# Regrouping products and visits at the start, one ScalarE step, and the conversion of w_out, in a fused retention and SiLU kernel

## The chip, the cores and the metric

The kernel runs on one core of a Trainium2 chip. The metric is the device time of one execution in microseconds; the median of 9 runs of the kernel before is 630.65 us (628.59 to 632.96). Profiles show one execution: TensorE is PE (its weight loads PEld), VectorE DVE, ScalarE ACT, GpSimd POOL, and SyncE (SP) issues most DMAs.

## What is computed

```python
for t in range(S):                       # B, H, S, D = 4, 8, 768, 64
    state = gamma[None, :, None, None] * state + einsum('bhd,bhe->bhde', k[:, :, t], v[:, :, t])
    y[:, :, t] = scale * einsum('bhd,bhde->bhe', q[:, :, t], state)
x = y.transpose(0, 2, 1, 3).reshape(B * S, H * D)      # 3072 x 512
h = x @ w_in                                           # 512 x 2048
out = (h * (1.0 / (1.0 + exp(-h)))) @ w_out            # 2048 x 512
```

The weights arrive as 64-bit floats and are converted in the kernel. Both large matrix products are made of three products of rounded parts (high by high, high by low and a mixed plane), so each has three planes of x or g and three of w.

## The kernel before

**Chunks and units.** The sequence of 768 is cut into NC = 6 chunks of 128 steps. A unit is one chunk of one batch, so there are 24 units, numbered chunk by chunk (unit 4c + b).

**Visits.** `visit(m)` (L535) works on three units at once. For unit m it transposes k and q on PE (`stage_t`, 8 transposes into the PSUM tiles kp and qp, copied out by ACT, L400). For unit m-1 it makes the chunk's sums of k and v (`stage_s`, L414) and the scores (`stage_a`, L424) in the PSUM tile sc. DVE then masks the scores (am, L432), adds up the state (mid, L441 and state, L445) and scales q (L365). For unit m-2 it makes y: the products with the masked scores first, then with the states, in two parts (`stage_y`, L457); a memset on POOL fences the two parts (`fence`). y is copied out of its one PSUM tile by ACT (ys, L492) and split into the three planes of xt (ACT L504, DVE L507, L508). At its end a visit issues the loads of later units on SP. From visit 2B + 1 = 9 on q and k of later units are loaded into rings of two or three buffers; from visit 17 the transposes run on DMA instead. One visit has 240 matmul and weight-load instructions for chunk 0 and 272 later.

**Products.** `product_in(c, f)` (L581) multiplies chunk c of x (all four batches, 512 columns) by slice f of 16 of w_in: 8 matmuls into ha and 4 into hb. ha and hb take turns on three PSUM banks, so hb of a product uses the bank of ha of the product before, and ha of a product that of hb two products before. Behind each product ACT copies ha into g (L589), DVE subtracts hb (L593, the product's sum), ACT applies SiLU (L597), and SP writes g to DRAM (gd). `behind_copy` and `behind_next` are lists of work that is issued behind a product's copy and behind its sum.

**Weights.** `take_w` converts the next of 32 slices (0 to 15 of w_in, 16 to 31 of w_out): ACT L197 (ca), DVE L199 (cs), L201 (ca), L204 (cs), L206 and L208 (cp), L214 (the sum cs, or cw for w_out). A slice of w_in is then split into three planes by `split_w`: ACT L119, DVE L122 (wil), ACT L124, DVE L125. A slice of w_out is written to DRAM (wod, L236), read back in the last group (wr, L622), and split there by `w_out` with the same four steps (wo, wol). The raw slices (wf, loaded two ahead, when the slice two before is converted) and the read-back slices (wr) share one ring of two tiles, `stage`; the tile wl serves both cw and wol. `begin_w` and `end_w` make the two halves of such a conversion inside the visits from 6 on.

**Order.** The order on PE is written by hand (L652 and after). On the other engines the order is fixed when the kernel is built, by the framework's scheduler, and each engine keeps it. By hand the order is: visits 0 to 9, with slice 0 taken behind visit 3, product (0,0) behind visit 7 and (0,1) behind visit 9; then the list `steps` of products, and in `behind` what follows each: visits 10, 11, 12 behind (1,0), (1,1), (1,2), visit 13 behind (1,3). Later visits stand behind every fourth product. Products of chunks 3, 4 and 5 make groups 3, 4 and 5. `takes` says behind which products slices are converted. A second phase (L718 and after) multiplies g, read back and split, by the planes of w_out: 6 chunks of 16 steps of 12 matmuls, 2.72 us a step.

Of the kernel before, what the change touches and what calls it, by code (L numbers as in the profile page):

```python
# [2 lines left out]

# [1 line left out]

# [27 lines left out]
def kernel(  # L33
# [29 lines left out]
    B, H, S, D = q.shape  # L63
# [5 lines left out]
    NF = DF // 128  # L69
# [43 lines left out]
    def split_w(f, w32, name, factor, to):  # L113


        to[f] = w = w_slot(f, name)
        lo = conv.tile([128, 512], FP32, tag="wl", name=f"{name}l_{f}")
        with tc.issue_after(held[0] if f >= NF - 4 else evac[0]):
            nc.scalar.activation(out=w[:, 0, :], in_=w32, func=AF.Copy, scale=HALF * factor)  # L119
        high = w[:, 0, :].bitcast(FP32)  # L120
        yield
        nc.vector.scalar_tensor_tensor(out=lo, in0=w32, scalar=factor, in1=high,  # L122
                                       op0=ALU.mult, op1=ALU.subtract)
        nc.scalar.activation(out=w[:, 1, :], in_=lo, func=AF.Copy, scale=1.0 / EPS)  # L124
        nc.vector.scalar_tensor_tensor(out=w[:, 2, :], in0=high, scalar=EPS, in1=lo,  # L125
                                       op0=ALU.mult, op1=ALU.subtract)


    units = [(c, b) for c in range(NC) for b in range(B)]
    kqv = {"k": {}, "q": {}, "v": {}}  # L130
    EARLY = 2 * B
# [90 lines left out]
    def take_w(after=None, parts=False):  # L222

        i = taken[0]
        taken[0] += 1
        if i >= 2 * NF:
            return
        with tc.issue_after(after) if after else ExitStack():
            rounded = convert_w(i)

        def finish():
            w32 = rounded()
            if i < NF:
                list(split_w(i, w32, "wi", scale, w_sb))
            else:
                nc.sync.dma_start(out=wo_dram[i - NF], in_=w32)  # L236

        if parts:
            behind_next.append(finish)
        else:  # L240
            with tc.issue_after(after) if after else ExitStack():
                finish()

    def end_w():

        while half_split:
            list(half_split.pop())
# [69 lines left out]
    behind_next, behind_copy, half_split = [], [], []  # L317
# [44 lines left out]
    def scale_q(n):  # L362
        c, b = units[n]
        t, g = (x if c > 0 else x[:, :, D:] for x in (qt[n], gq))
        nc.vector.tensor_tensor(out=t, in0=t, in1=g, op=ALU.mult)  # L365
# [25 lines left out]
    def stage_t(n):  # L391

        for name, to, bufs, src, tp in (
                ("kt", kt, 2, kqv["k"][n], turn(f"kp_{n}")),
                ("qt", qt, 3, kqv["q"].pop(n), banks("q", f"qp_{n}", 1)[:, 0])):
            tp = tp.rearrange("p (a t) -> p a t", a=HP)
            for a in range(HP):
                nc.tensor.transpose(tp[:, a, :], src[:, 2 * a : 2 * a + 2, :], ident)  # L398
            to[n] = one.tile([128, HP, C], FP32, tag=name, name=f"{name}_{n}", bufs=bufs)
            evac[:] = [nc.scalar.copy(out=to[n], in_=tp).ins]  # L400

    def score_tile(n):
        u = banks("s", f"sc_{n}")
        sc, sums = (u[:, :, ts(i, 4 * D)].rearrange("p o (a t) -> p o a t", a=HP)
                    for i in range(2))
        return sc, sums
# [40 lines left out]
    def stage_y(n):  # L447

        vs, amn, qtn = kqv["v"].pop(n), am.pop(n), qt.pop(n)
        states = steps_of.pop(n)  # L450
        yp = banks("y", f"y_{n}")[:, :, : 4 * D].rearrange("p o (a t) -> p o a t", a=HP)

        started, done, new = set(), [], []

        def product(a, o, j, lhsT, rhs):
            e = j ^ (a % 2)
            i = nc.tensor.matmul(yp[ts(e, D), o, a, :], lhsT=lhsT, rhs=rhs,  # L457
                                 start=(e, o) not in started, stop=True,
                                 skip_group_check=True).ins
            started.add((e, o))  # L460
            if new:
                fence(done[-1], i)
                new.clear()
            done.append(i)

        def scores():
            for a in range(HP):
                for o in range(2):
                    for j in range(2):
                        product(a, o, j, vs[ts(o, D), 2 * a + j, :], amn[ts(o, D), j, a, :])  # L470

        def states_with(part):

            new.extend([part] * part)
            for a in range(HP):
                for o in range(2):
                    j = o ^ part
                    if states[o] is not None:
                        product(a, o, j, states[o][ts(j, D), a, :], qtn[ts(j, D), a, ts(o, D)])

        return scores, states_with, yp
# [52 lines left out]

    def visit(m):  # L535

        first, mid, last = (0 <= m - i < len(units) for i in range(3))
        if first and m < FAR:
            stage_t(m)
        if last:  # L540
            scores, states_with, yp = stage_y(m - 2)
            scores()
        if mid:
            sc, sums = score_tile(m - 1)
            stage_s(m - 1, sums)
        if last:
            states_with(0)
        if mid:
            stage_a(m - 1, sc)
            if m > 1 and units[m - 1][1] == 0:  # L550
                next_chunk()

            with tc.issue_after(taken_out[0]) if m > 3 * B + 1 else ExitStack():
                finish_a(m - 1, sc, sums)
            scale_q(m - 1)
        if m == 0:
            chunk_decays()
            first_chunk()
        if first and m < FAR:
            scale_k(m)  # L560
        if last:
            states_with(1)
            finish_y(m - 2, yp)

        if FAR <= m < len(units):
            with tc.issue_after(fenced[0]):
                part_t(m)
        for name in "kqv":
            for n in (m + 1, m + 2):
                if n >= EARLY and n == (m + 1 if name == "v" or n > FAR else m + 2):  # L570
                    load(name, n)
        if EARLY - 2 <= m < 3 * B + 2:
            with tc.issue_after(masked[0]):
                end_w()
                if m not in (EARLY - 1, EARLY + 1):
                    begin_w()
# [4 lines left out]
    def product_in(c, f):  # L581
        ha, hb = turn(f"ha_{c}_{f}"), turn(f"hb_{c}_{f}")
        for i in range(3):
            for kk in range(KIN):
                nc.tensor.matmul(hb if i == 2 else ha, lhsT=w_sb[f][:, i, ts(kk, 128)],  # L585
                                 rhs=xt[c][:, i, kk, :], start=kk == 0 and i != 1,
                                 stop=kk == KIN - 1 and i != 0)
        hs = hpool.tile([128, NT], FP32, tag="hs", name=f"g_{c}_{f}")
        copied[:] = [nc.scalar.activation(out=hs, in_=ha, func=AF.Copy, scale=ONE_E).ins]  # L589
        with tc.issue_after(copied[0]):  # L590
            while behind_copy:
                behind_copy.pop(0)()
        taken_out[:] = [nc.vector.tensor_tensor(out=hs, in0=hs, in1=hb, op=ALU.subtract).ins]  # L593
        with tc.issue_after(taken_out[0]):
            while behind_next:
                behind_next.pop(0)()
        nc.scalar.activation(out=hs, in_=hs, func=AF.Silu)  # L597
        pending.append((c, f, hs))
# [52 lines left out]

    ctx.enter_context(tc.manual_schedule(engines={mybir.EngineType.PE}))  # L652

    for m in range(EARLY + 2):
        visit(m)
        if m == 3:
            take_w()
        elif m == EARLY - 1:
            load_w(3)
            product_in(0, 0)  # L660
        elif m == EARLY + 1:
            product_in(0, 1)

    half = NF // 2
    pairs = [(1, 0), (1, 1)] + [(c, f) for f in range(2, 4) for c in range(2)]
# [3 lines left out]
    last = ([(c, f) for c in range(2) for f in range(NF - 4, NF)] +  # L669
            [(2, f) for f in range(half, NF)])  # L670
    groups = [(c, f) for c in range(3, NC) for f in range(NF)]
    steps = pairs + three + rest + last + groups
    takes = [(0, f) for f in range(5, half)]
    takes += [(2, half - 4), (2, half - 2)]
    takes += [(0, half), (0, half + 2), (1, half), (1, half + 2)]
    takes += [(0, NF - 4), (0, NF - 2), (2, half + 2), (2, half + 4)]
    takes += [(c, f) for c in (3, 4) for f in (0, 3, 6, 8, 11, 14)]
    behind = {(1, f): lambda f=f: visit(EARLY + 2 + f) for f in range(3)}
    behind[1, 3] = lambda: [visit(3 * B + 1), behind_next.append(end_w)]
    at = ([(1, NF - 1)] + [(2, f) for f in range(NF - 7, NF - 2, 2)] +  # L680
          [(c, 4 * i + 1) for c in range(3, NC - 1) for i in range(B)])
# [36 lines left out]
    for c in range(NC):  # L718
# [8 lines left out]
        for f in range(NF):  # L727
# [5 lines left out]
            first_, last = f == 0, f == NF - 1  # L733
# [57 lines left out]
```

## Time and profile before

| | us |
|---|---|
| median of 9 runs | 630.65 |
| the profiled execution | 630.81 |
| its span, first to last instruction | 629.0 |

Busy time in stretches of the span:

| stretch | what runs | PE busy | DVE busy | ACT busy |
|---|---|---|---|---|
| 0 to 66 | visits 0 to 10, three products | 49.49 | 45.61 | 42.92 |
| 66 to 132 | visits 11 to 13, products | 65.74 | 58.08 | 51.40 |
| 132 to 205 | products, the first late visits | 72.37 | 62.96 | 44.94 |
| 205 to 318 | late visits, groups 3 and 4 | 111.54 | 91.85 | 69.25 |
| 318 to 362 | group 5 | 44.00 | 33.60 | 34.49 |
| 362 to 629 | second phase | 262.27 | 133.61 | 68.97 |

In the first stretch PE is idle for 16.5 us, in all others together for 7. The granted clock of PE is full but for one window in the first stretch. A line of the chain of waits gives start, length, and the work or wait that carried the end; a line of a stretch gives for each engine its busy time and, behind x, its instructions.

### The profile page before, as it was taken

Reading aid. Unit: us, or ns where it says so; the run is one execution under the profiler, and the core shown is the slowest. Engines: PE = TensorE matmul, PEld = TensorE weight load, DVE = VectorE, ACT = ScalarE, POOL = GpSimd, SP = SyncE. Lnnn points to the kernel's source line nnn. Section 1 sums busy time; section 2 is a strip of 40 time slices with the busy share of each in tenths; the row PEclk is TensorE's granted clock in tenths of the full one; section 3 lists DMA queues with packets and bytes.
Section 4 is the critical chain, followed back from the end, with each engine's and each line's share of the span. In section 5 each row is a group of like instructions: output and inputs, shape, how many; then the busy total and the mean of one; then the engine's idle time right before and its main releaser. Section 6 shows DMA issues by size and latency. Waiting matters only on the chain.

```text
span 629.0 us, 13483 instructions
## 1 busy us (share of the span) xinstructions
PE 605.4 (96%) x5384; PEld 499.8 (79%) x5384; DVE 425.7 (68%) x732; ACT 312.0 (50%) x583; POOL 23.4 (4%) x79
## 2 busy tenths in 40 slices
PE   5788999999999999999999999999999999999997
PEld 3677788887888787888788888888888888888785
DVE  2798898798978888897697583553636454554631
ACT  5567896666655566667478761312312221412211
POOL 3000000000000211111000000000000000000000
PEclk9998999999999999999999999999999999999999
DMA  9996887445667799999856553342533433432301
GB/s 199 209 212 165 225 231 228 168 150 192 196 202 200 191 271 252 258 269 263 290 188 207 178 168 100 119 149 68 169 99 106 163 95 106 136 132 96 106 1 67
DMA packets 137998, 107.31 MB, mean 171 GB/s; under 512 B 94800, under 2 KB 103248, under 8 KB 137936
## 3 DMA queue, kind: packets, MB, share of 16 engines
q1 hardware_dynamic: 135056, 101.21, 57.0%
q10 hardware_dynamic: 2880, 5.24, 2.2%
q8 instruction: 42, 0.69, 0.5%
q14 instruction: 20, 0.16, 0.1%
HBM read 66.06 MB, written 36.70 MB: 163 GB/s over the span
## 4 chain that ended last, share of the span: by engine, by line
PE 84%; DVE 6%; DMA 3%; issue 2%; ACT 2%; SPq 2%; DVEq 0%; ACTq 0%; POOLq 0%
PE ha L585 23%; PE o L740 20%; PE oa L740 14%; PE hb L585 12%; PE ob L740 7%; PE y L457 4%; PE sc L424 1%; PE sc L414 1%; SPq L149 1%; PE qp L398 1%; DMA qw<-qp 1%; DMA kqv<-in_q_dram 1%; DMA wf<-in_moe_w_in_dram 1%; PE kp L398 1%; DMA wod<-cw 1%
## 5 line engine op out<-in xcount | busy, mean ns | idle before, releaser
L585 PE MATMUL ha<-xt,wi 128*128 128x512 f32 x768 | 192.7, 393 | 0.0
L585 PEld LDWEIGHTS ha<-xt,wi 128*128 128x128 f32 x768 | 142.8, 188 | 30.9 <-DVE g L593 0.4
L740 PE MATMUL o<-wo,gs 128*128 128x512 f32 x576 | 146.2, 389 | 0.0
L740 PEld LDWEIGHTS o<-wo,gs 128*128 128x128 f32 x576 | 108.1, 188 | 22.4
L642 DVE TENSOR_TENSOR gs<-gr,gs 128x512 fp32r<-128x512 f32 x96 | 62.1, 685 | 90.8 <-ACT gs L640 90.8
L640 ACT ACTIVATE gs<-gr 128x512 fp32r<-128x512 f32 x96 | 53.4, 621 | 134.7 <-issue 132.3
L740 PE MATMUL oa<-wo,gs 128*128 128x512 f32 x384 | 118.2, 389 | 0.0
L585 PE MATMUL hb<-xt,wi 128*128 128x512 f32 x384 | 103.1, 390 | 1.5 <-ACT g L589 1.4
L593 DVE TENSOR_TENSOR g<-g,hb 128x512 f32<-128x512 f32 x96 | 65.6, 683 | 36.7 <-ACT g L589 23.2
L585 PEld LDWEIGHTS hb<-xt,wi 128*128 128x128 f32 x384 | 71.8, 188 | 17.7 <-ACT g L589 2.2
L740 PEld LDWEIGHTS oa<-wo,gs 128*128 128x128 f32 x384 | 72.1, 188 | 14.9
L597 ACT ACTIVATE g<-g 128x512 f32<-128x512 f32 x96 | 60.5, 631 | 41.8 <-DVE g L593 41.6
L740 PE MATMUL ob<-wo,gs 128*128 128x512 f32 x192 | 75.2, 392 | 0.3 <-DVE o L749 0.3
L589 ACT ACTIVATE g<-ha 128x512 f32<-128x512 f32 x96 | 56.6, 589 | 25.7 <-PE ha L585 12.1
L643 DVE SCALAR_TENSOR_TENSOR gs<-gs 128x512 fp32r<-128x512 f32 x96 | 61.9, 683 | 0.0
L740 PEld LDWEIGHTS ob<-wo,gs 128*128 128x128 f32 x192 | 36.0, 188 | 9.3 <-DVE o L749 2.0
L197 ACT ACTIVATE ca<-wf 128x512 f32<-128x512 f32 x32 | 21.6, 676 | 16.0 <-DVE cs L204 6.1
L208 DVE SCALAR_TENSOR_TENSOR cp<-wf,cp 128x512 f32<-128x512 uint32 x32 | 23.5, 734 | 0.6
L457 PE MATMUL y<-qt,mid 64*64 64x64 f32 x384 | 21.9, 230 | 2.0 <-issue 2.0
L204 DVE SCALAR_TENSOR_TENSOR cs<-ca,cs 128x512 uint32<-128x512 uint32 x32 | 22.1, 690 | 0.9
L748 ACT ACTIVATE o<-o 128x512 f32<-128x512 f32 x10 | 6.0, 598 | 33.4 <-PE o L740 33.0
L432 DVE TENSOR_TENSOR am<-sc,decay 128x512 f32<-128x512 f32 x24 | 16.4, 684 | 8.8 <-PE sc L424 8.7
(84 smaller groups left out, 557.9 us busy)
## 6 DMA issues: line engine op xcount, KB each, us to landing
gd<-g SPq DMA_DIRECT2D x96, 256.0 KB, 3.1
gr<-gd SPq DMA_DIRECT2D x96, 256.0 KB, 2.7
wf<-in_moe_w_out_dram SPq DMA_DIRECT2D x16, 512.0 KB, 4.4
out_dram<-o ACTq DMA_DIRECT2D x20, 256.0 KB, 2.1
wf<-in_moe_w_in_dram SPq DMA_DIRECT2D x16, 256.0 KB, 3.9
wf<-in_moe_w_in_dram SPq DMA_DIRECT2D x32, 128.0 KB, 4.0
kf<-in_k_dram SPq DMA_DIRECT2D x16, 256.0 KB, 4.8
qf<-in_q_dram SPq DMA_DIRECT2D x16, 256.0 KB, 4.3
```

The costliest lines, as they stand in the source:

```text
L197: nc.scalar.activation(out=a.bitcast(FP32), in_=hi.bitcast(FP32), func=AF.Abs, scale=65536.0)
L204: nc.vector.scalar_tensor_tensor(out=s, in0=a, scalar=3, in1=s, op0=ALU.logical_shift_left, op1=ALU.bitwise_or)
L208: nc.vector.scalar_tensor_tensor(out=p.bitcast(FP32), in0=lo, scalar=2.0 ** -52, in1=p.bitcast(FP32), op0=ALU.mult, op1=ALU.mult)
L457: i = nc.tensor.matmul(yp[ts(e, D), o, a, :], lhsT=lhsT, rhs=rhs, start=(e, o) not in started, stop=True, skip_group_check=True).ins
L585: nc.tensor.matmul(hb if i == 2 else ha, lhsT=w_sb[f][:, i, ts(kk, 128)], rhs=xt[c][:, i, kk, :], start=kk == 0 and i != 1, stop=kk == KIN ...
L589: copied[:] = [nc.scalar.activation(out=hs, in_=ha, func=AF.Copy, scale=ONE_E).ins]
L593: taken_out[:] = [nc.vector.tensor_tensor(out=hs, in0=hs, in1=hb, op=ALU.subtract).ins]
L597: nc.scalar.activation(out=hs, in_=hs, func=AF.Silu)
L640: nc.scalar.activation(out=t[:, 0, :], in_=g, func=AF.Copy, scale=HALF)
L642: nc.vector.tensor_tensor(out=t[:, 1, :], in0=g, in1=high, op=ALU.subtract)
L643: nc.vector.scalar_tensor_tensor(out=t[:, 2, :], in0=t[:, 1, :].bitcast(FP32), scalar=-1.0 / EPS, in1=high, op0=ALU.mult, op1=ALU.add)
L740: nc.tensor.matmul(o, lhsT=g, rhs=wo[f][:, i, :], start=first_ and i != 1, stop=last and i != 0)
```

## The change

Four edits. A visit is written as a generator of two halves, `halves(m)`: the first has the transposes, y's products with the scores and the first part of those with the states; the second has the rest. In every visit `stage_s` thereby moves behind the first part of the states. The start is reordered: slice 0 is taken behind visit 2 instead of 3, product (0,0) stands behind visit 6 instead of 7, and from visit 9 halves and products alternate: 9a, (0,1), 9b, 10a, (1,0), 10b, (1,1), 11a, (0,2), 11b, (1,2), 12a, (0,3), 12b, (1,3), 13. The step to the next chunk's decay (`next_chunk`, four ACT operations) is issued, in late visits, behind the copy of the next product and a unit earlier. And slices are taken behind other products: four of w_in's and all of w_out's, whose last twelve are spread over groups 3, 4 and 5 as 5, 4 and 3 instead of over groups 3 and 4 as 6 and 6.

```diff
     def visit(m):
+        list(halves(m))
+    def halves(m):
         first, mid, last = (0 <= m - i < len(units) for i in range(3))
         if first and m < FAR:
             stage_t(m)
         if last:
             scores, states_with, yp = stage_y(m - 2)
             scores()
+            states_with(0)
+        yield
         if mid:
             sc, sums = score_tile(m - 1)
             stage_s(m - 1, sums)
-        if last:
-            states_with(0)
-        if mid:
             stage_a(m - 1, sc)
-            if m > 1 and units[m - 1][1] == 0:
+            if 1 < m <= 3 * B + 1 and units[m - 1][1] == 0:
                 next_chunk()
...
             scale_q(m - 1)
+            if m > 3 * B + 1 and units[m - 1][1] == B - 1:
+                behind_copy.append(next_chunk)
...
-    for m in range(EARLY + 2):
+    for m in range(EARLY + 1):
         visit(m)
-        if m == 3:
+        if m == 2:
             take_w()
+        elif m == EARLY - 2:
+            product_in(0, 0)
         elif m == EARLY - 1:
             load_w(3)
-            product_in(0, 0)
-        elif m == EARLY + 1:
-            product_in(0, 1)
+    half_visits = (x for m in range(EARLY + 1, 3 * B + 1) for x in chain(halves(m), (None,)))
+    next(half_visits)
+    product_in(0, 1)
+    next(half_visits)
+    next(half_visits)
...
-    takes += [(0, half), (0, half + 2), (1, half), (1, half + 2)]
-    takes += [(0, NF - 4), (0, NF - 2), (2, half + 2), (2, half + 4)]
-    takes += [(c, f) for c in (3, 4) for f in (0, 3, 6, 8, 11, 14)]
-    behind = {(1, f): lambda f=f: visit(EARLY + 2 + f) for f in range(3)}
+    takes += [(0, half), (0, half + 3), (1, half + 1), (1, half + 3)]
+    takes += [(0, NF - 2), (2, half), (2, half + 2), (2, half + 4)]
+    takes += [(3, f) for f in (0, 3, 7, 11, 14)]
+    takes += [(4, f) for f in (3, 7, 11, 14)]
+    takes += [(5, f) for f in (1, 3, 5)]
+    behind = {x: lambda: next(half_visits) for x in pairs[:-1]}
```

More of the change, by code (lines that the diff above doesn't have):

```diff
@@ L2 @@
 from contextlib import ExitStack
+from itertools import chain
 import numpy as np
```

## The prediction

> **What bounds the kernel now.** The page comes first: 605.4 us of TensorE (PE) in 629.0, and the slices where it is short are the first six or seven of forty.
>
> ```profile
> PE 605.4 (96%) x5384; PEld 499.8 (79%) x5384; DVE 425.7 (68%) x732; ACT 312.0 (50%) x583; POOL 23.4 (4%) x79
> ...
> PE   5788999999999999999999999999999999999997
> ...
> PEclk9998999999999999999999999999999999999999
> ...
> q8 instruction: 42, 0.69, 0.5%
> ```
>
> So the change can win only what PE idles, some 24 us in all, over half of it before 66 us. Next the chain of waits of that stretch, for what PE waits for there:
>
> ```profile
> 34.72 1.12 issue
> ...
> 39.18 1.43 issue
> ...
> 48.45 1.72 issue
> ...
> 59.99 1.16 PE hb L585 x4
> ...
> 63.61 1.12 issue
> ```
>
> "issue" means that no semaphore explains the wait. The table of stretches, cut in these gaps, says what does:
>
> ```profile
> 35.00:40.00 5.00, 3.34 (x127) 2.87 (x126) 4.31 (x9) 3.00 (x6) 0.09 (x1) 1.00 0.89 209
> 40.00:49.50 9.50, 7.84 (x253) 6.89 (x254) 9.50 (x19) 5.12 (x9) 0.18 (x2) 1.00 0.93 210
> 49.50:64.00 14.50, 13.34 (x252) 10.81 (x252) 11.67 (x22) 11.74 (x31) 0.09 (x1) 0.88 0.59 153
> 64.00:89.00 25.00, 24.07 (x508) 20.64 (x508) 23.16 (x45) 22.05 (x58) 0.35 (x4) 1.00 0.84 225
> 48.39:51.80 3.41, 1.69 (x42) 1.32 (x41) 3.27 (x7) 2.01 (x4) 0.00 (x0) 1.00 0.80 174
> 51.80:55.20 3.40, 3.40 (x113) 3.28 (x106) 2.98 (x6) 3.30 (x11) 0.09 (x1) 0.50 0.32 74
> ```
>
> Matmuls and weight loads between two gaps number 253, 507, 504 and 1016: once, twice, twice and four times one block. Queue 8 brings 42 packets of 0.69 MB/42 = 16 KB for 10,768 such instructions, 256 each. The gaps are PE waiting for its code. A visit holds 272 instructions and needs about 3.2 us without a gap (68.4 to 71.6), but consecutive blocks came 4.76 us apart (35.84 to 40.60): visits back to back are short by about 1.5 us. A product has 24 instructions and 2.72 us, so a block with one in it is on time (none is late in visit 8, behind product (0,0)).
>
> **A rule against the change.** The Trainium skill ("Runtime: NRT & Kernel Launch", Instruction fetch mechanics) holds that crossing a 16 KiB boundary is mostly hidden. By it these four gaps (5.4 us) have another cause and regrouping visits wins nothing; by the rows they sit on every such boundary and a product in the block removes them. I go by the rows. "TensorE: Matmul & The Clock Gate" (Part 1) lets the clock fall to half after an idle window of about 3.4 us; here a window with 1.69 of 3.41 us busy was followed by 3.40 us at 0.50, costing about 1.5 us. By the rule a gap under 3.4 us is free, by the row one of 1.7 us can cost as much again.
>
> **Start, visits 2 to 13.** *Slice 0's conversion behind visit 2.* Its five operations on VectorE (DVE), start to start in the timeline 0.33 + 0.61 + 0.44 + 0.60 + 0.60 = 2.6 us, ran between 22.1 and 27.4; now they stand ahead of visit 2's mask (am), for which DVE had been idle 2.97 us before 18.47. ACT's first step (0.7) can start when visit 2's copy of qt ends, 16.3, so they end at 19.65: the mask is 1.2 us late, visit 3's scores 0.8. In return DVE is that much freer in visits 4 and 5, where PE waited for it:
>
> ```profile
> PE y L457 <- DVE am L432: 1.7, 2, 1.1
> PE sc L414 <- DVE state L445: 1.7, 3, 1.0
> ```
>
> Little of it arrives. Visit 5's q let PE start only at 28.92; visit 6's q, issued at 27.71, lands about 5 us later (median 5.1); and blocks keep their distance. I let visit 6's gap end at 35.2 instead of 35.84: -0.6 (between 0 and the 3.2 us of both rows).
>
> *Product (0,0) behind visit 6.* The rest of visit 6 took 1.75 us behind its gap, so it ends at 36.95 and the product at 39.7; its xt was complete at 36.7, and the last third is needed 1.8 us in. Visit 7's block is in time now: the gap of 1.43 goes, visit 7 ends at 43.1. But visits 7 and 8 now adjoin. Visit 8's y needs the one PSUM tile y, which ACT must first copy out; in the new order that copy stands behind slice 1's first plane, and this behind DVE's sum of (0,0), four steps of the conversion and k's scaling: 39.75 + 0.6 x 5 + 0.34 and their hand-overs is 43.9; plane and copy, 0.6 each: 45.15, against 46.30. The next block is 4.76 us behind, 49.9 against 50.17, after a gap of 1.65. Most of the lead is lost here.
>
> *Halves.* From there each half has a product beside it. A first half is 112 instructions (1.4 us; 1.9 for 9a, which starts from an empty engine), a second 160 (1.95): 9a to 51.8, (0,1) to 54.5, 9b to 56.45, 10a to 57.9, (1,0) to 60.85 (0.2 of waiting for xt's last third, 0.6 before), 10b to 62.8. Product (1,1) starts at 62.8 against 65.65: **-2.85**. In it are the gap at 63.61 (1.12), the half clock (1.5) and the rest of the lead. If the half clock returns behind the gap of 1.65, the gain is 1.35. After that visits and products take turns as before: DVE, idle 3.52 us before 65.47, has room; what is late next is a product's sum, now ahead of the visit's mask, by up to 0.6 us, with 1.4 us of transposes between mask and use. Loads on SP leave with the second half, 2.7 us later: visit 11's q, issued at 53.43, has some 10 us until its use.
>
> **Decay term behind a copy, and order in the visit.** Four ACT operations of 0.33 us move and four are added at the end; ACT is 50% busy and the product's copy is ahead of them: 0, at most +0.3. The sums now run after the first half of the state products, so PE's one wait for the POOL fence (0.30 at 312.2) is covered: -0.3.
>
> **w_out's slices.** Takes lie 3, 2, 2 products apart in place of 2, 2, 2, and the doubles (3,6)/(3,8), (4,6)/(4,8) are gone. With them go the waits at 148.6 (0.63, ACT's copy behind an unlanded slice) and this:
>
> ```profile
> 251.67 1.21 PE L585 MATMUL hb<-xt,wi 128*128 128x512 f32 x4 [0.75 <-ACT g L589]
> ```
>
> -1.4 together. The price is in group 5, where three takes meet the first reloads (wr). Both use the ring wf of two tiles, so reload 1 waits until slice 30's last read (L208) is done. Before, the same hand-over:
>
> ```profile
> 320.71 0.68 DVE L208 SCALAR_TENSOR_TENSOR cp<-wf,cp 128x512 f32<-128x512 uint32 x1
> ...
> 321.42 0.32 SPq L622 DMA_DIRECT2D wr<-wod  x1
> ...
> DMA to landing us min/median/max: 2.5/2.8/4.0
> ```
>
> There nobody needed it at once. In the new order that read stands behind the sum of (5,5): it ends 2.95 us after that product (0.7 for the sum, then cs, cs, cp and cp, 2.25 with their hand-overs); issue to landing 2.6; ACT's first plane 0.6; and only then, queued behind it on ACT, the copy of (5,6), 0.6: 6.98 with hand-overs. Product (5,7) needs the bank for hb at 2.72 + 1.81 = 4.53: **+2.45** (2.0 to 3.9 by the landing's extremes). SP is held too: g of (5,4), slice 29's write and the next reload queue behind reload 1, which makes the later copies ready 0.0–0.5 us before need; I add 0.3. The last reloads run into the second phase, where slice 12 is due 32 us in: 0.
>
> **Sum** against the profiled execution, 630.81 (span 629.0 and 1.8 around it, 0.16 over the median): -2.85 - 0.3 - 1.4 + 2.45 + 0.3 = -1.8, so 629.0.
>
> **Cases** (0.2%, about what this kernel's measurement can tell, is 1.26 us).
> A, as summed: 629.0, 628.0 to 630.2; 0.42, of it 0.28 faster and 0.14 within.
> B, the wait at (5,7) doesn't come, because reload 1 lands early or the tile order differs from my reading: 626.3; 0.18. For it: ACT waited only 0.7 us for reloads before. Against: the order is fixed when the kernel is built.
> C, the start brings 1.35, the gap of 1.65 drawing the half clock again: 630.5; 0.22, mostly within. This is also the case in which regrouping only moves the code waits.
> D, slower: the ring hand-over stalls at each of the three takes of group 5, since a late DVE or SP leaves no slack for the next: 3 x 2.45 - 4.55 = +2.8, 633.6; 0.18. It decides from 5.6 us of PE idleness in group 5.
> Range 626.2 to 632.4: A, B and C, and part of D.
>
> **What would show it.** After: no "issue" gap at visits 7 and 10, one of about 1.65 before visit 9; (1,1) starting near 62.8; PEclk without a half window; no wait at (1,9) and (3,9); in group 5 one wait of about 2.5 us of hb for ACT's copy, with the ACT row of wo waiting for wr just before. Wrong if blocks come at another pace, or if PE shows no gap in group 5.

## The result, and the profile after

The changed kernel takes 628.04 us (median of 17 runs, 626.11 to 630.24); the kernel before, run beside it, 630.96 (54 runs). The ratio is 0.995 with a 95% interval of 0.9937 to 0.9963, so it is 2.3 to 4.0 us, 0.4 to 0.6%, faster. Beside the kernel before on other chips it came to 0.9948 (0.9930 to 0.9966) and 0.9943 (0.9925 to 0.9961). The profiled execution has a span of 626.4 us in place of 629.0. The page's PE row, its slices and the clock (one digit for each fortieth of the span):

```profile
PE 603.5 (96%) x5384; PEld 496.4 (79%) x5384; DVE 424.6 (68%) x732; ACT 314.3 (50%) x587; POOL 21.8 (3%) x79
...
PE   5887999999999999999999999999999999999997
...
PEclk9999999999999999999999999999999999999999
```

The slices of the start are hardly fuller than before. In the chain of waits (start, length, what carried the end) VectorE now carries the end for 7.4 us between visits 6 and 8, through slice 1's conversion to the copy of y:

```profile
29.74 0.34 issue
...
33.61 1.06 issue
...
36.24 0.69 DVE am L433
...
42.96 0.70 DVE cs L215
...
44.31 0.48 ACT ys L493
...
46.96 3.20 issue
...
64.18 2.04 PE ha L592 x8
```

The last line is product (1,1), at 65.65 in the chain before. The gaps in visits 7 and 10 are gone, but at the end of visit 8, where 1.65 was forecast, 3.20 stand, and one more is in PE's rows of visit 8's transposes, where the chain runs over VectorE:

```profile
44.15 0.44 PE L399 MATMUL qp<-ident,qf 128*128 128x128 f32 x2 [0.62 <-issue]
```

So PE again has four "issue" gaps at block boundaries: 0.34, 1.06, 0.62 and 3.20, 5.2 us together, where the four of the kernel before were 5.4. The reordering moved them and hardly shortened them. Now the two traces laid side by side, by when the same product starts on PE:

| start of | before | after | difference | change since the row above |
|---|---|---|---|---|
| (1,1) | 65.58 | 64.11 | -1.47 | -1.47 |
| (1,5) | 100.36 | 100.43 | +0.07 | +1.54 |
| (3,0), group 3 | 211.19 | 209.98 | -1.21 | -1.28 |
| (4,0), group 4 | 265.94 | 263.02 | -2.92 | -1.71 |
| (5,0), group 5 | 318.43 | 315.10 | -3.33 | -0.41 |
| second phase | 361.95 | 359.34 | -2.61 | +0.72 |
| end | 629.02 | 626.42 | -2.60 | 0 |

The whole lead of the start is lost again by product (1,5). The lead itself is not steady: two more profiles of the changed kernel start (1,1) at 64.48 and 66.57, while the two experiments that keep the old start have it at 65.48 and 65.72. All that is left at the end was won between 100 and 318 us, where the slices and the decay term moved. By the profile the sum is -2.6 in place of -1.8, but it is made of other terms.

### The profile page after: what moved, and what is told of

Its sections match the earlier page's. It is cut to its first block, busy times and chain, and to the rows that moved or that the text cites. A ratio compares the mean times of both kernels' runs of the same rounds, so it can differ in the third digit from the quotient of the medians.

```text
span 626.4 us, 13485 instructions
## 1 busy us (share of the span) xinstructions
PE 603.5 (96%) x5384; PEld 496.4 (79%) x5384; DVE 424.6 (68%) x732; ACT 314.3 (50%) x587; POOL 21.8 (3%) x79
## 4 chain that ended last, share of the span: by engine, by line
PE 84%; DVE 5%; SPq 4%; DMA 3%; issue 2%; ACT 2%; DVEq 0%; ACTq 0%; POOLq 0%
PE ha L592 25%; PE o L754 21%; PE oa L754 14%; PE hb L592 12%; PE ob L754 7%; PE y L458 3%; SPq L150 3%; PE sc L425 1%; PE sc L415 1%; DMA wr<-wod 1%; DMA kw<-kp 1%; DMA kqv<-in_q_dram 1%; PE qp L399 1%; PE kp L399 0%; DVE g L600 0%
## 5 line engine op out<-in xcount | busy, mean ns | idle before, releaser
L458 PE MATMUL y<-qt,mid 64*64 64x64 f32 x384 | 20.2, 221 | 0.0
L763 DVE TENSOR_TENSOR o<-o,o 128x512 f32<-128x512 f32 x10 | 6.8, 687 | 19.3 <-ACT o L762 19.3
```

## Experiments

**The edits one by one.** Three kernels, each with one part of the change. *start_only* is the changed kernel with the old `takes` and `next_chunk`; *takes_only* is the kernel before with the new list:

```diff
-    takes += [(c, f) for c in (3, 4) for f in (0, 3, 6, 8, 11, 14)]
+    takes += [(3, f) for f in (0, 3, 7, 11, 14)]
+    takes += [(4, f) for f in (3, 7, 11, 14)]
+    takes += [(5, f) for f in (1, 3, 5)]
```

(and the new places of w_in's slices and of w_out's first four); *chunk_only* is the kernel before with `behind_copy.append(next_chunk)`.

> The changed kernel with the slices and the decay term as before: only the start (slice 0 behind visit 2, product (0,0) behind visit 6, halves, sums behind the first part of the states). Theory D (VectorE is the bound from about 64 to 98 us, so a lead at (1,1) is given back by product (0,5)): (1,1) starts about 1.5 us earlier, (1,5) within 0.3 us of before, and the time is within 0.2% of before (-0.3 to +0.3 us). Theory P (the prediction: the lead is kept): 1.3 to 2.9 us faster than before.

> The kernel before with only the other list of slices. Theory D (all of the gain comes from the slices): -2.0 to -3.0 us, with the waits for ACT's copy near 148 and 251 us gone and +0.5 to +0.8 us in group 5. Theory P (the start brings half of it or more): -0.3 to -1.4 us.

> The kernel before with only the decay term moved behind a product's copy and one unit earlier. By the prediction 0 (at most +0.3 us). The rival: it is what removes the 0.41 us in which PE waits for ACT's copy of kt at 218 us; then -0.3 to -0.6 us and that wait is gone, while it stays if the slices removed it.

Against the kernel before on the same chip: start_only 1.0011 (0.9997 to 1.0026), takes_only 0.9945 (0.9928 to 0.9963), chunk_only 0.9987 (0.9974 to 1.0000). The start alone brings nothing, and the slices alone are as fast as the whole change. The decay term alone brings something between nothing and 1.6 us. The profiled execution of start_only (636.93) was the slowest of its 22, and (1,1) was late in it (66.93, against the expectation), so it has no lead that could be seen to be lost; but from (1,1) to (1,5) it needs 36.28 us, as the changed kernel does (36.32), where the kernel before needs 34.78.

chunk_only's profile shows that one of my two waits had two causes. It no longer has the wait at 250.92, though slices are still taken behind (3,6) and (3,8). The chain of the kernel before, cut to that stretch, tells why:

```profile
242.64 4.68 DMA wod<-cw
...
247.42 1.17 DVE cw L214
248.59 0.60 DVE am L432
...
249.52 0.61 DVE qt L365
...
250.46 0.68 ACT gq L312 x2
251.14 0.48 ACT g L589
...
251.67 0.98 PE hb L585 x3
```

Read from the top: the sum cw of one slice cannot be written until the last slice's DMA out of the same tile has landed (4.68 us); the mask and the scaling of q stand behind it on DVE; the decay term waits for that scaling; and the product's copy stands behind the decay term on ACT. The chain is broken either by more products between two slices or by putting the decay term behind the copy. Each edit alone removes the wait (takes_only has none there either); together they remove it once. In chunk_only's profile this gains 1.9 us in group 3 (52.87 in place of 54.74), but group 4 is 1.4 longer (53.93 in place of 52.49, with new waits of 0.32 and 0.37 for ACT's copies), and its span, 629.2, is no shorter than before. What brings these waits was not looked into.

**Is it the spread over three groups?** *six_six* is the changed kernel with the last twelve slices back at six and six:

```diff
-    takes += [(3, f) for f in (0, 3, 7, 11, 14)]
-    takes += [(4, f) for f in (3, 7, 11, 14)]
-    takes += [(5, f) for f in (1, 3, 5)]
+    takes += [(c, f) for c in (3, 4) for f in (0, 3, 6, 8, 11, 14)]
```

> The changed kernel with the last twelve slices of w_out back in groups 3 and 4, six each, as before; decay term, slices of w_in and start as changed. If the gain in the groups comes from spreading the slices over three groups: 1.0 to 2.5 us slower than the changed kernel, with waits of hb for ACT's copy near 250 us or behind unlanded slices. If the decay term (which stood ahead of a product's copy on ACT) and w_in's slices made it: equal or 0.7 us faster, since the late product in group 5 (+0.56) goes.

0.9986 (0.9971 to 1.0001), beside the changed kernel's 0.9948 on that chip: 2.4 us slower, with intervals that do not meet. So by the times the spread is the larger part of the gain, even with the decay term moved. Where the waits are, ACT's timeline of six_six shows (start, busy time, instruction, and in brackets the idle time ahead of it and what ended it):

```profile
255.47 1.37 ACT L389 COPY qt<-qw 128x1024 uint16<-128x1024 uint16 x1 [0.83 <-DMA qw<-qp]
256.70 1.32 ACT L389 COPY kt<-kw 128x1024 uint16<-128x1024 uint16 x1
```

PE's scores (sc) waited 0.88 us for that kt. q's copy waited for its transposition by DMA; a product's copy ahead of it, at 254.04, had waited 1.74 us for a write of g to DRAM. Both transfers are issued by SP, whose queue also carries the slices' loads and writes. Groups 3 and 4 took 53.93 and 52.97 us, the changed kernel's on the same chip 52.95 and 52.08. Group 5, which has no slices in six_six, took 43.57 against 44.73, so the two profiles differ by only 0.7 us in the three groups; the 2.4 us rest on the medians of 14 and 6 runs.

**Why the start's lead is lost.** VectorE's row between (1,1) and (1,5), before and after (columns as in the prediction's table of stretches):

```profile
65.58:100.36 34.78, 34.52 (x522) 29.18 (x517) 33.62 (x64) 30.98 (x75) 0.27 (x3) 1.00 0.91 248
```

```profile
64.11:100.43 36.32, 35.71 (x523) 28.54 (x517) 33.91 (x64) 31.85 (x75) 0.27 (x3) 1.00 0.79 227
```

The same 64 operations fill 33.62 of 34.78 us before: there were 1.2 us of room. After, they fill 33.91 of 36.32, and most of the 2.4 us of idleness is in three rows:

```profile
71.92 0.69 DVE L600 TENSOR_TENSOR g<-g,hb 128x512 f32<-128x512 f32 x1 [1.22 <-ACT g L596]
72.98 0.69 DVE L433 TENSOR_TENSOR am<-sc,decay 128x512 f32<-128x512 f32 x1 [0.38 <-PE sc L425]
81.94 0.69 DVE L433 TENSOR_TENSOR am<-sc,decay 128x512 f32<-128x512 f32 x1 [0.38 <-PE sc L425]
```

In the kernel before, the mask of visit 11 (72.08) follows slice work without a pause, its scores being ready. In the new order the scores come with the second half, behind product (0,2), and this product's sum stands ahead of the mask: VectorE runs dry early in the stretch and is behind at its end. *relief* takes 3.2 us of its work out of the stretch (58 operations in place of 64; the expectation had 4.7): visit 13 begins no slice, and slices 6 to 9 are converted later.

```diff
-                if m not in (EARLY - 1, EARLY + 1):
+                if m not in (EARLY - 1, EARLY + 1, 3 * B + 1):
...
-    takes = [(0, f) for f in range(5, half)]
+    takes = [(2, 0), (2, 1), (1, 6), (1, 7)]
```

> The changed kernel in which visit 13 begins no slice: slice 6 is converted behind product (2,0), slices 7, 8 and 9 behind (2,1), (1,6) and (1,7), so that about 4.7 us of VectorE's work leave the stretch before product (2,0). If VectorE bounds this stretch (theory D): the wait of 0.60 us for the sum at 93.6 us goes, (1,5) starts 0.8 to 1.4 us earlier than in the changed kernel, and the time falls by as much unless the later slices give it back. If the lead is lost to something else (the bank turns, the code): (1,5) stays at 100.4, no change in time.

> The changed kernel, unaltered, beside the next three on one chip, since chips differ by more than the edits do. By its first result a ratio of 0.993 to 0.997 to the kernel before.

> The changed kernel, unaltered, to compare the next two with on one chip: ratio to the kernel before 0.993 to 0.997.

> The run with relief once more, beside the changed kernel. If VectorE's room between (1,1) and (1,5) is worth something at the end: 0.5 to 1.3 us faster than the changed kernel, the stretch from (1,1) to (1,5) being 35.3 us in place of 36.3. If the time that it wins is given back: within 0.3 us of the changed kernel.

In the changed kernel DVE's timeline just before product (2,0) is one unbroken row, with the sum of (0,4) in it, and PE's first matmul waits for that. Of what stands ahead of the sum, ca and cs belong to the slice that visit 13 begins:

```profile
92.21 0.42 DVE L202 TENSOR_SCALAR ca<-ca 128x512 f32<-128x512 f32 x1
...
93.15 0.42 DVE L200 TENSOR_SCALAR cs<-wf 128x512 uint32<-128x512 uint32 x1
93.49 0.68 DVE L600 TENSOR_TENSOR g<-g,hb 128x512 f32<-128x512 f32 x1
...
94.22 2.40 PE L592 MATMUL ha<-xt,wi 128*128 128x512 f32 x8 [0.60 <-DVE g L600]
```

This wait of 0.60 us is in all seven profiles with the new start and visit 13's slice, and those need 36.28 to 36.37 us from (1,1) to (1,5). It is in none of the four with relief (one of them cover_relief, below), which need 35.19 to 35.59. relief's row:

```profile
65.34:100.65 35.31, 35.05 (x522) 28.92 (x517) 30.75 (x58) 29.78 (x73) 0.26 (x3) 1.00 0.78 225
```

By the chain of waits VectorE carries the end from 85.1 to 94.2 us in the changed kernel; in the kernel before PE carries all of it. So VectorE bounds the end of this stretch, and relief gets back 0.7 to 1.2 us of the 1.5. Its 35.19 to 35.59 are not quite the 34.78, 34.93 and 35.32 of the three profiles with the old start (before, chunk_only, takes_only); what the rest is was not separated. In time, relief measured 0.9924 (0.9902 to 0.9946) at first, and 0.9940 (0.9924 to 0.9957) beside the changed kernel's 0.9943: no difference that can be told. Of the 1.0 to 1.1 us won, 0.4 go again before group 3 (109.9 us from (1,5) to (3,0), against 109.6), and the rest is under what such a comparison resolves. The second half of the first expectation, a fall in time, was not shown.

**Are the issue gaps the code?** *shift* puts 64 small matmuls ahead of visit 0, *shift_half* 32; their result is not used:

```diff
+    dummy = banks("s", "dummy")
+    for _ in range(32):
+        nc.tensor.matmul(dummy[:D, 0, :D], lhsT=ident[:, :D], rhs=ident[:, :D],
+                         start=True, stop=True, skip_group_check=True)
     for m in range(EARLY + 1):
         visit(m)
```

> The changed kernel with 64 small matmuls into an unused tile ahead of visit 0 (128 instructions more on PE with their weight loads, while it waits for the first loads anyway; their result is not used). If the issue gaps are PE's wait for the next 256 instructions: every gap moves 128 instructions earlier in the work, so the one of visit 6 comes half a visit earlier (in its transposes or in visit 5's end), and the one at the end of visit 8 comes among visit 8's transposes and y, always at instruction 194 + 256 n of the whole sequence. If something in the visits causes them (an unseen dependence on ACT or VectorE): they stay at the same instruction of the work, y of visit 6 and the end of visit 8. Time: 0 to +2 us.

> As the run called shift, but with 32 such matmuls: in that run each was recorded as two, so that 64 of them and their weight loads made 256 instructions, one whole block, and every boundary fell on the same work as before. 32 make 128, half a block. If the issue gaps are PE's wait for the next 256 instructions: they come at instruction 194 + 256 n of the new count, so 128 instructions earlier in the work, half a visit: not at y of visit 6 and not at the end of visit 8, but in the sums and scores of a visit. If the visits cause them: at y of visit 6 and at the end of visit 8, as in the changed kernel.

shift told nothing: each fp32 matmul was recorded twice, its weight load too, so that 256 instructions, one whole block, were added and every boundary fell on the same work again (gaps at the same y's). With half a block the gaps moved by half a visit. PE's rows in visit 6, the changed kernel and then shift_half:

```profile
32.92 0.68 PE L458 MATMUL y<-am,kqv 64*64 64x64 f32 x29
34.67 0.27 PE L458 MATMUL y<-am,kqv 64*64 64x64 f32 x2 [1.06 <-issue]
```

```profile
35.73 0.41 PE L425 MATMUL sc<-qt,kt 64*64 64x64 f32 x13
39.36 0.79 PE L425 MATMUL sc<-qt,kt 64*64 64x64 f32 x18 [3.22 <-issue]
```

With PE's own wait instructions counted too, the two gaps of shift_half stand at instructions 1218 and 1474 of the new count, 194 + 256 n both, among the scores of visits 5 and 6; visit 6's y and visit 8's end have none. The visits do not cause them; the block boundary does. (The times of the two, 0.9987 and 0.9985, contain the added work.)

*cover_relief* was meant to put a product into the block that ends with the gap of 3.20 (relief's edits are in it too):

```diff
-    for m in range(EARLY + 1):
+    for m in range(EARLY - 1):
         visit(m)
...
-    half_visits = (x for m in range(EARLY + 1, 3 * B + 1) for x in chain(halves(m), (None,)))
+    half_visits = (x for m in range(EARLY - 1, 3 * B + 1) for x in chain(halves(m), (None,)))
+    next(half_visits)
+    product_in(0, 0)
+    next(half_visits)
+    load_w(3)
+    next(half_visits)
     next(half_visits)
     product_in(0, 1)
-    next(half_visits)
-    next(half_visits)
+    for _ in range(3):
+        next(half_visits)
```

> The changed kernel with two edits: slices 6 to 9 converted later as in the run with relief, and visits 7 and 8 in halves too, so that the order is 7a, (0,0), 7b, 8a, 8b, (0,1), 9a, 9b, 10a, (1,0): a product among every 1.6 visits. If PE waits for its code (blocks of 256 instructions): the issue gap of about 3 us at the end of visit 8 shrinks to 0.5 to 1.5 us, a smaller one of up to 1 us comes in visits 9 and 10, (1,1) starts 1 to 2 us earlier than in the changed kernel, and with relief for VectorE this lead stays to (1,5): 1.5 to 3 us faster than the changed kernel. If VectorE bounds the start already from 38 us on: the gap moves but (1,1) stays within 0.5 us of 64.1 to 65.3, and the time is that of relief alone.

It did not: the gaps are 1.11 in visit 6, 1.91 in visit 7 and 2.52 at the end of visit 8. The boundaries stand at 35.55, 40.71, 46.31 and 51.58, and (0,0), at 41.32, lies in the block before the one that was meant. That block, with the product, ends without a gap; the blocks on both sides of it, with visits alone, end with one. This is what the prediction said of blocks, but whether a product in the last of them would shorten its gap was not tried. (1,1) starts at 65.42, and the time is 0.9952 (0.9934 to 0.9971), no better than the changed kernel's.

**Group 5.** *relief_552* takes one slice from group 5 to group 4:

```diff
-    takes += [(3, f) for f in (0, 3, 7, 11, 14)]
-    takes += [(4, f) for f in (3, 7, 11, 14)]
-    takes += [(5, f) for f in (1, 3, 5)]
+    takes += [(c, f) for c in (3, 4) for f in (0, 3, 7, 11, 14)]
+    takes += [(5, f) for f in (1, 3)]
```

> Relief, and the last twelve slices of w_out spread as 5, 5 and 2 over groups 3, 4 and 5 in place of 5, 4 and 3, which takes the last of them away from the reloads in group 5. If the hand-over of the ring costs 0.5 to 0.7 us in group 5: that goes, and it is up to 0.7 us faster than relief alone, unless the fifth slice in group 4 brings a wait of its own. If group 4 is the tighter one: equal to relief alone or slower by up to 0.7 us.

0.9961 (0.9941 to 0.9981): no gain. Group 5 took 45.04 us, and 0.54 of it were one wait of hb for ACT's copy at 355.1, long after the last slice. Three profiles of the changed kernel itself have 43.52, 44.24 and 44.73 us, where 16 products of 2.72 are 43.52. What group 5 loses differs between executions from nothing to 1.2 us; neither theory said that. Nor is it the slices there alone: start_only, which has none in group 5, took 44.49.

## Where the prediction was right and wrong, step by step

- *PE waits for its code.* Right, and shown by shift_half. From the first half of visit 9 on, where halves and products alternate, no block boundary has a gap before (1,1), as forecast. The rule of the Trainium skill ("Runtime: NRT & Kernel Launch", Instruction fetch mechanics), that crossing is mostly hidden, does not hold in these dense stretches. The pace was too regular: I took 4.76 us a block, measured were 3.9 to 6.0 in the changed kernel (6.7 in shift_half), so the gap of 1.65 was 3.20 (2.62 and 2.37 in its other profiles). I counted a block from visit 8's y at 45.15; the boundary was in the transposes before it, at 44.15.
- *Half clock.* The gap of 3.20 us drew no half window, while that of 1.72 in the kernel before drew one. Counted in steps of 3.41 us from the half window that this trace has at 14.50 to 17.91, the gap lay astride two windows with 1.7 and 1.9 us of work. In the third profile of the same kernel and in relief the gap at this place (2.37 and 2.92) drew one. Whether another 1.7 us are lost is a matter of where the gap falls. The half window at 14.50 lies across two slices, so that the row of nines does not show it. It makes no difference between the kernels: four transposes take 1.06 us at 14.46 in the one and 1.08 at 14.62 in the other, and 0.60 in both from 19 us on.
- *Slice 0, product (0,0).* Near: visit 3's y waited 0.95 (0.8), the mask coming 1.25 us later than before (1.2), visit 6's gap ended at 34.67 (35.2), (0,0) began at 36.33 (36.95), visit 8's y at 44.84 (45.15).
- *Halves: (1,1) at 62.8, -2.85 kept to the end.* This step failed, twice. The size: -1.47 in this profile, by the larger gap, and no steady lead in others, since the issue gaps at block boundaries up to (1,1) are 5.2, 7.5 and 6.3 us together in the three profiles of the changed kernel against 5.4, 5.1 and 4.6 in those with the old start. Case C had named this: regrouping only moves the code waits. And its sequel, "DVE, idle 3.52 us before 65.47, has room": 1.47 us of lead came to a stretch in which VectorE had 1.2 us of idleness in 34.78, and by (1,5) nothing was left. I read one idle gap at the stretch's head in place of the busy share of the stretch, which the same table had. start_only's time agrees: 1.0011. I had the product's sum ahead of the mask, and put its cost at up to 0.6 us with room to spare; the three rows above are 2.0 us of idleness.
- *Decay term, 0 to +0.3.* Not settled. It takes the wait at 251 away, which I had not seen, but chunk_only's span is 0.2 us longer than before, and its time (0.9987) is anything from nothing to 1.6 us faster.
- *Fence, -0.3.* Wrong: the 0.30 are at 308.84 as they were at 312.16. It is the last visit, which has no next unit's sums to cover the fence with.
- *Slices, -1.4.* Right in kind, mis-sized: the two waits went, and with them others, -1.28, -1.71 and -0.41, 3.4 us in all with the decay term. The cause I gave the second wait (two slices close together) was one of two.
- *Ring in group 5, +2.75.* Wrong in place and size: +0.72. SP's reloads 1 and 2 in the changed kernel (reload 0 left at 325.81, when slice 29 had left its tile):

```profile
330.28 0.32 SPq L629 DMA_DIRECT2D wr<-wod  x1
...
334.65 0.32 SPq L629 DMA_DIRECT2D wr<-wod  x1
```

  and the DVE operations that released them:

```profile
329.57 0.68 DVE L123 SCALAR_TENSOR_TENSOR wol<-wr,wo 128x512 f32<-128x512 f32 x1
...
333.93 0.69 DVE L209 SCALAR_TENSOR_TENSOR cp<-wf,cp 128x512 f32<-128x512 uint32 x1
```

  Reload 1 left at 330.28, right behind reload 0's own split (ended 330.25), from the tile that slice 29 had left; slice 30 kept the other tile until 334.6 and held reload 2. I had reload 1 behind slice 30. That is case B. The wait that I had described came three products later, at (5,10), and smaller: ACT's first plane of a later reload waited for its landing, and the copy behind it was late for hb:

```profile
342.85 0.63 ACT L120 ACTIVATE wo<-wr 128x512 fp32r<-128x512 f32 x1 [1.71 <-DMA wr<-wod]
...
344.54 1.21 PE L592 MATMUL hb<-xt,wi 128*128 128x512 f32 x4 [0.23 <-ACT g L596]
```

  start_only has the same wait at (5,10), 0.61 us, without a slice in group 5, and the third profile of the changed kernel has none. (The range of 2.0 to 3.9 was not the working's either: landings of 2.5 to 4.0 in place of 2.6 give 2.35 to 3.85.)

The misses add to +2.9 (start), +0.3 (fence), -2.0 (slices) and -2.0 (ring), -0.8 together. That the time came near the forecast is luck: the losses and gains that I missed nearly cancel.

## What to carry to other kernels

A lead on one engine lasts only as far as the next stretch in which another engine is nearly full: before counting a gain, take the busy share of every other engine from there to the end, not the idle time just ahead. Add up the gaps of the same kind before and after: here a gap that went came back elsewhere. Work that runs beside the bound (converting weights) is worth spreading until none of it queues ahead of the step that the bound waits for; here that was the gain. And a wait with two sufficient causes must not be booked once for each edit that removes it.

## What the hardware showed beside this

PE takes its instructions in blocks of 256: 256 more left the gaps at the same work, 128 more moved them by 128. In the changed kernel's start the packet of the next block (queue 8) appears 1.1 to 3.1 us after the first instruction of a block and takes 1.0 to 1.6 us, and where PE stood idle it went on 1.4 to 1.6 us after the packet's end. What delays the packet by up to 3.1 us (the DMA engines moved data 0.96 of the time then) was not tried. Half-clock windows are 3.41 us long and followed windows of that length in which the trace has PE busy for 0.4 to 1.9 us; but windows with 1.5 to 2.0 were also followed by full clock, so the trace gives no sharp bound. Matmuls of fp32 operands are recorded twice, those of fp32r once. And the same changed kernel started (1,1) at 64.11, 64.48 and 66.57 us in three profiles: the start differs between executions by more than this change moved it.
